# A block of the most frequent expert of the first half, gathered during attention and computed in the router's stretch

## The chip, the cores and the metric

The kernel runs on one core of a Trainium2 chip. The metric is the device time of one execution in microseconds (us). Five engines work side by side, each on its own list of instructions in order: TensorE (PE, matrix products; loads of its stationary operand are PEld), VectorE (DVE), ScalarE (ACT), GpSimd (POOL) and SyncE (SP), which here only issues transfers (DMA) and reads registers. Products land in PSUM banks; all else on the chip is in SBUF.

## The reference

Three parts in a row, in float32:

- Attention with rotary embedding for 2 batches, 8 heads, 576 positions, 64 columns a head. Its output is x, 1152 tokens of 512 columns; the first batch is tokens 0 to 575.
- A mixture of 8 experts, each token to one: `expert_idx = argmax(xn @ en.T / tau)` with normalized rows, `h = relu(x @ w1[e])` (512 to 1024), `out = gate * (h @ w2[e])` (1024 to 512), the gate being the softmax value of the chosen expert.
- A dense layer pair on the result: `x @ w_in` (512 to 2048), softplus, `@ w_out` (2048 to 512); both weights come in float64.

Products are made in three terms: an operand is split into a rounded part (hi) and the rest (lo), and hi*hi, hi*lo and lo*hi are summed. So each weight tile of 128x1024 costs a rounding copy (ACT) and a subtraction (DVE), and each activation tile likewise.

## The kernel before

**Attention.** Heads go in eight pairs j (0 to 3 are batch 0, 4 to 7 batch 1), nine steps g to a pair, t = 9j + g. The loop over t (L747) writes out the order of every engine: in step t ACT makes the exponential of tile t, PE transposes tile t-1, multiplies scores of tile t+2, and then does the step's `fill` (products with V, transposes for the next pair), which takes one or two of the two PSUM banks of `ps_m`; the evictions of these banks come in step t+1. POOL makes the rotary embedding of pair j+2 in pair j, up to pair 5. Small pieces of router work are let into the loop with generators (`next(rgen0)`).

**The router.** A token's expert is the first maximum of its 8 values; these are known for batch 0 after pair 3 and for batch 1 only at the end. From one-hot rows PE counts how many tokens of the same expert stand before each (`rank_mm`, `rank_before`, `count_mm`), `places` and `sequence` turn that into a block and a row in it, and `at_places` puts the token's number at its place with small products. Each expert gets blocks of 128 tokens, in the order of experts; `eid` and `chg` tell each block's expert and whether it is a new one.

**The blocks.** NU = 13 blocks are always worked on; with more, a branch does the rest. A block is: `gather(n)` (POOL: an indirect DMA of its rows from the copy `xs` of x in HBM), four transposes (`x_t`) and the split (`x_ev`), `layer1(n)` (24 products of 128x512), `relu(n)`, eight transposes (`h_t`) and the split (`h_ev`), `layer2(n)` (24 products), the gate's scaling (`y_row`) and the scatter to `ys` (`y_put`). Weights come in eight pieces of 512 KB a block; `split_w` rounds one on ACT, subtracts on DVE and issues the next block's fetch of that piece on SP. Blocks 0 to 3 are written out by hand (L1194 on), the others come from `run`; in four of them a piece of the dense stage's first weights is decoded (`between`, `decode`), and in the last ones finished rows of `ys` are read back and transposed (`y_t`).

Block 0 always belongs to expert 0, so its w1 is fetched and split by POOL in pairs 6 and 7 (`first_weights`). The router's stretch itself goes from the end of attention to block 0's first layer; between the router's small products PE multiplies ones with ones (`warm`, 138 products). In it POOL gathers block 0 as soon as its tokens' places are known, after both parts of `x_store(1, ...)` (batch 1's rows to `xs`: six heads' columns, then the last two heads').

**Queues.** All loads, weight fetches and stores of x are issued by SP in the order of the program; one that waits holds those behind it. Gathers and scatters are issued by POOL, between its other work. The expert stage's tiles lie where attention's were, and a tile's first write waits until the last reader of what lay there is done.

Of the kernel before, what the change touches and what calls it, by code (L numbers as in the profile page):

```python
# [33 lines left out]
NBLK = 2 * E  # L34
# [7 lines left out]
WARM0, WARM1, WARM2, WARM3, WARM4, WARM5 = 28, 22, 28, 36, 40, 12  # L42
# [9 lines left out]
def table():  # L52
# [12 lines left out]
    put("ev", np.arange(E)[None, :])  # L65
# [30 lines left out]
def moe_kernel(ctx: ExitStack, tc: tile.TileContext, q, k, v, emb, tau, w1, w2, w_in, w_out, rope, tab, out):  # L96
# [18 lines left out]
    rp = actx.enter_context(tc.tile_pool(name="rp", bufs=2))  # L115
    acon = actx.enter_context(tc.tile_pool(name="acon", bufs=1))
# [13 lines left out]
    zero = acon.tile([P, 2, 2 * P], F32, name="zero")  # L130
    V.memset(zero, 0.0)
# [49 lines left out]
    def first_max(b):  # L181
# [15 lines left out]
        if b == 0:  # L197
            both.update(oh=w([P, B * 5, E], "oh", BF16), j=w([P, B * 5], "j", I32), first=w([P, B * 5, 1], "first", F16), mask=w([P, B * 5, NBLK], "mask"), gm=w([P, B * 5, NBLK], "gm"))
        oh = rb[b]["oh"] = both["oh"][:, 5 * b:5 * b + 5]
        V.tensor_tensor(oh, rev, bc(mx, E, 2), op=ALU.is_equal)  # L200

    def rank_before(pr):

        for c in range(5):
            T.matmul(pr, lhsT=ones, rhs=bc(rb[0]["oh"][:, c], 5, 1), start=(c == 0), stop=False)

    def rank_mm(b, pr):

        oh = rb[b]["oh"]
        T.matmul(pr, lhsT=upper, rhs=oh, start=(b == 0), stop=False)  # L210
# [3 lines left out]
    def count_mm(b, pc):  # L214
        for c in range(5):
            T.matmul(pc, lhsT=ones, rhs=rb[b]["oh"][:, c], start=(b == 0 and c == 0), stop=(b == 1 and c == 4))

    def places(b, pr):
# [5 lines left out]
        ri = w([P, 5], f"ri{b}", I32)  # L224
# [15 lines left out]
        G.tensor_copy(rb[b]["row"], row)  # L240

# [30 lines left out]
    def sequence(pcnt, cnt, q):  # L272
# [26 lines left out]
        V.tensor_tensor(chg[:, 1:NBLK], ef[:, 1:NBLK], ef[:, 0:NBLK - 1], op=ALU.not_equal)  # L299
        V.tensor_copy(cnt, pcnt)  # L300
        V.scalar_tensor_tensor(nblk, nov[:, E - 1:E], 1.0, st[:, E - 1:E], op0=ALU.add, op1=ALU.add)

    def destinations(cnt, q):
# [11 lines left out]
        V.tensor_tensor(dest, base, skip, op=ALU.add)  # L315

    firsts = {}

    with actx:
# [14 lines left out]
        for t in qzs:  # L334
            G.tensor_copy(t, zero)
# [7 lines left out]
        def load(*js, between=()):  # L343
            for j in js:
                loaded[j] = (ld.tile([P, 2, 9, D], F32, tag="qk", name="qk"), ld.tile([P, 10, D], F32, tag="vv", name="vv"))
# [81 lines left out]
        def prep(j):  # L427
            if j not in prepped:
                prepped[j] = (hp.tile([P, 2, S], F32R, tag="kt", name="kt"), hp.tile([P, 2, 2, 512], F32R, tag="qt", name="qt"), qzs[j % 2])
# [50 lines left out]
        def first_weights(cs):  # L480

            for c in cs:
                raw = ld.tile([P, FF], F32, tag="qk", name="raw0")
                hi, lo = (rp.tile([P, FF], F32R, tag=t, name="part0") for t in (("t1", "t1"), ("t2", "t2"), ("ks", "qq"), ("ks", "qq"))[c])
                SY.dma_start(raw, w1[0, P * c:P * c + P])
                firsts[c] = (hi, lo)
                yield
                for x in range(4):
# [4 lines left out]
                    yield  # L493

# [63 lines left out]
        def ev_lo(t):  # L558
# [180 lines left out]

        vgen = v_first()  # L740
# [6 lines left out]
        for t in range(NS + 5):  # L747
# [72 lines left out]
            if (j, g) == (6, 1):  # L820
                wgen = first_weights((0, 1, 2))
                for _ in range(2):
                    next(wgen)
            if (j, g) == (7, 0):
                for _ in wgen:
                    pass
                wgen = first_weights((3,))
            for _ in range(4):
                next(wgen, None)
            if (j, g) == (6, 0):  # L830
                zsum(0)
                rgen0 = first_max(0)
            if (j, g) == (7, 1):
                pr0 = ps_m.tile([P, 5, E], F32, tag="m", name="pr0")
                rank_mm(0, pr0)
                rgen0 = places(0, pr0)
            elif g:
                next(rgen0, None)
# [636 lines left out]
```

## Time and profile before

| | |
|---|---|
| median of 3 runs | 574.09 us (573.15 to 574.10) |
| the profiled execution | 574.03 us, its span 572.3 us |
| granted TensorE clock, mean | 0.995 |
| busy PE, DVE, ACT, POOL | 544.2, 448.8, 440.1, 202.6 us |
| attention, to about | 183 us |
| the router's stretch | 183.7 to 194.4 us |
| the 13 blocks | 194.4 to 361.8 us |
| the dense stage | 362.9 us to the end |

Busy time counts an instruction from its start to its modelled end; products overlap, so that a stretch in which PE is marked busy throughout can still go faster. The time from one instruction's start to the next one's is the better measure, and it is what the rows of the timeline give.

### The profile page before, as it was taken

To read this page: it belongs to the slowest core of one execution; us is meant where nothing else is said; L and a number is where in the kernel's file an instruction comes from. 1 tells how busy PE (TensorE), PEld (TensorE's weight loads), DVE (VectorE), ACT (ScalarE), POOL (GpSimd) and SP (SyncE) were. 2 spreads that over 40 slices of the span, in tenths; PEclk is the share of its full clock that TensorE was granted. 3 is DMA by queue.
4 is the path that set the end of the run, shared out by engine and by line. 5 is a ranking of instruction groups with operands and counts; after the bars stand their busy time and mean duration, and the time that the engine had idled before them with its cause. 6 is when DMAs were issued, how large, how long until landed. Compare 5 with 4: busy or idle time off the path is not lost. (4 is left out here: it accounts for less than half of the span.)

```text
span 572.3 us, 10066 instructions
## 1 busy us (share of the span) xinstructions
PE 544.2 (95%) x3361; PEld 477.2 (83%) x3361; DVE 448.8 (78%) x747; ACT 440.1 (77%) x838; POOL 202.6 (35%) x314
## 2 busy tenths in 40 slices
PE   6799999999999999998999999899999999999995
PEld 6689899999988888887778888797889999888994
DVE  6788887878977779989999998687877766787243
ACT  4787878887775599799998988788877877676550
POOL 7999999849731420332222412300000000000033
PEclk9899999999999999999999999999999999999999
DMA  5405200061143655982539895453332222000012
GB/s 143 123 2 151 67 1 3 0 221 38 38 169 116 199 163 174 316 300 71 216 102 333 290 377 174 133 191 102 107 112 74 77 80 71 33 1 2 0 74 92
DMA packets 37431, 70.61 MB, mean 123 GB/s; under 512 B 8306, under 2 KB 24050, under 8 KB 37248
## 3 DMA queue, kind: packets, MB, share of 16 engines
q1 hardware_dynamic: 34400, 62.66, 33.1%
q0 software_dynamic: 2800, 7.09, 3.6%
q8 instruction: 28, 0.46, 0.3%
q10 hardware_dynamic: 176, 0.18, 0.2%
q14 instruction: 27, 0.22, 0.1%
HBM read 91.14 MB, written 8.13 MB: 173 GB/s over the span
## 5 line engine op out<-in xcount | busy, mean ns | idle before, releaser
L966 DVE TENSOR_TENSOR wt<-raw,wt 128x1024 fp32r<-128x1024 f32 x100 | 116.4, 1221 | 5.8 <-ACT wt L962 5.8
L1336 PE MATMUL ph<-yt,wt 128*128 128x320 f32 (+1 forms) x576 | 105.4, 336 | 2.5 <-ACT r__5876 L1348 1.4
L1383 PE MATMUL po<-wt,g 128*128 128x512 f32 x432 | 103.6, 391 | 0.0
L1336 PEld LDWEIGHTS ph<-yt,wt 128*128 128x128 f32 x576 | 93.5, 188 | 11.8 <-ACT r__5876 L1348 1.8
L962 ACT CAST wt<-raw 128x1024 fp32r<-128x1024 f32 x100 | 98.8, 1066 | 5.5 <-DMA raw<-in_moe_w_dram 5.5
L1383 PEld LDWEIGHTS po<-wt,g 128*128 128x128 f32 x432 | 80.4, 188 | 16.7 <-ACT g L1367 0.3
L1030 PE MATMUL py<-wt,ht 128*128 128x512 f32 x312 | 75.7, 395 | 3.8 <-DVE wt L966 3.8
L1400 POOL DMA_INDIRECT out_dram<-acc,otok x9 | 9.6, 1067 | 186.2 <-DVE acc L1397 185.6
L1030 PEld LDWEIGHTS py<-wt,ht 128*128 128x128 f32 x312 | 57.5, 188 | 16.6 <-DVE wt L966 5.1
L1001 PE MATMUL ph<-wt,xt 128*128 128x512 f32 x288 | 69.1, 394 | 0.0
L543 ACT ACTIVATE p<-sc,nm 128x576 f32<-128x576 f32 x72 | 54.0, 750 | 11.6 <-DVE nm L537 10.7
L1001 PEld LDWEIGHTS ph<-wt,xt 128*128 128x128 f32 x288 | 53.1, 188 | 10.6
L537 DVE TENSOR_REDUCE nm<-sc 128x1 f32<-128x576 f32 x72 | 54.1, 752 | 3.1 <-PE sc L533 1.9
L556 ACT CAST ph<-tp 128x512 fp32r<-128x512 f32 (+1 forms) x80 | 42.8, 547 | 13.5 <-PE tp L549 13.0
L533 PE MATMUL sc<-kt,qt 128*128 128x288 f32 x256 | 50.4, 319 | 0.8 <-ACT p L543 0.4
L567 DVE TENSOR_TENSOR pl<-tp,ph 128x512 fp32r<-128x512 f32 (+1 forms) x80 | 49.5, 628 | 0.1
L379 POOL TENSOR_TENSOR t<-qk,ropet 128x256 f32<-128x256 f32 x61 | 43.7, 744 | 10.6 <-DMA qk<-in_q_dram 10.2
L549 PE MATMUL tp<-idf,p 128*128 128x128 f32 x288 | 44.8, 278 | 1.8 <-DVE jz L233 0.6
L1367 ACT CAST g<-e 128x512 fp32r<-128x512 f32 (+2 forms) x33 | 21.6, 658 | 29.6 <-PE po L1383 20.2
L1368 DVE TENSOR_TENSOR g<-e,g 128x512 fp32r<-128x512 f32 (+2 forms) x33 | 24.3, 740 | 23.7 <-ACT g L1367 23.5
L594 PE MATMUL po<-ph,vs 128*128 128x288 f32 x128 | 36.4, 307 | 2.2 <-DVE p L435 1.3
L533 PEld LDWEIGHTS sc<-kt,qt 128*128 128x128 f32 x256 | 36.7, 192 | 1.8 <-ACT p L543 1.1
(246 smaller groups left out, 1001.7 us busy)
## 6 DMA issues: line engine op xcount, KB each, us to landing
raw<-in_moe_w_dram SPq DMA_DIRECT2D x116, 512.0 KB
raw<-in_moe_w_in_dram SPq DMA_DIRECT2D x16, 512.0 KB
raw<-in_moe_w_out_dram SPq DMA_DIRECT2D x16, 512.0 KB
yr<-ys SPq DMA_DIRECT2D x9, 256.5 KB
qk<-in_k_dram SPq DMA_DIRECT2D x8, 256.0 KB
qk<-in_q_dram SPq DMA_DIRECT2D x8, 256.0 KB
vv<-in_v_dram SPq DMA_DIRECT2D x8, 256.0 KB
xs<-xrow SPq DMA_DIRECT2D x1, 1024.0 KB
```

What stands on the lines that cost most here:

```text
L379: eng.tensor_tensor(t[:, i, g], x4[:, i, g], ropet[:, m, 0:4].unsqueeze(2).to_broadcast([P, 4, 2, 32]), op=ALU.mult)
L533: T.matmul(sc[:, n, 0:288], lhsT=w, rhs=r, start=(x == 0), stop=(x == len(mm) - 1))
L537: V.tensor_reduce(nm, tiles['sc', t][:, :, 0:288], axis=AX.XY, op=ALU.max, negate=True)
L543: A.activation(p.rearrange("p (n t) -> p n t", n=2), tiles.pop(('sc', t))[:, :, 0:288], AF.Exp, bias=tiles.pop(('nm', t)), accum_out=head( ...
L549: T.transpose(tp[:, x], p[:, x * P:x * P + P], idf)
L567: V.tensor_tensor(hd['pl'][:, :, sl], tp[:, :, x * w:x * w + w], f(hd['ph'][:, :, sl]), op=ALU.subtract)
L962: A.copy(wt[:, 0], raw)
L966: (eng or V).tensor_tensor(wt[:, 1], raw, f(wt[:, 0]), op=ALU.subtract)
L1001: T.matmul(ph[i], lhsT=xt[:, a, c], rhs=wt[:, r, 512 * i:512 * i + 512] if n else wt[r][:, 512 * i:512 * i + 512], start=(c == 0 and a == ...
L1030: T.matmul(py, lhsT=ht[c // 2][:, a, k], rhs=rhs[:, s], start=(c == 0 and r == 0 and a == 0 and s == 0), stop=(c == 3 and r == 1 and a == 1))
L1336: T.matmul(phs[i][:, 0:n1 - n0], lhsT=wt[:, a, k], rhs=yts[p][:, r, k, n0:n1], start=(k == 0 and a == 0 and r == 0), stop=(k == 3 and a == 1))
L1383: T.matmul(outs[i][c], lhsT=g[:, a, c * P:c * P + P], rhs=wt[:, r], start=(first and a == 0 and r == 0), stop=(last and a == 1))
```

## The change

The most frequent expert of batch 0 alone is found in pair 5 (`most`): its first 128 tokens (or as many as there are) become block 0, and the others are ranked as if these weren't there (`rank_shift`, and a term in `count_mm`). NBLK is 17, the remaining blocks are numbered from 1, and NU stays 13.

In pairs 6 and 7 the block's tokens are placed (`choose`) and gathered, its rows transposed (`x_first`), and w1 of that expert and three quarters of its w2 are fetched by a register and split by POOL (`first_weights(l, cs)`); the last quarter of w2 is fetched and split in the router's stretch. There both layers run (`layer1_x`, `layer2_x`), in place of `warm`. Block 1 (expert 0) follows; its weights are split like any other block's. Part of the gates' squares moves into the last steps of attention.

Pools are laid out anew: the K and Q tiles have a pool `hq`, V's loads `lv`; w2's pieces use the K and Q tiles (`hq`), the block's rows V's.

```diff
+    def most(pc):
+        m0 = w([P, 1], "m0x")
+        V.tensor_reduce(m0, pc, axis=AX.X, op=ALU.max)
...
+        V.tensor_scalar(both["ox"], rev[:, 0], mx, m0, op0=ALU.is_equal, op1=ALU.mult)
...
+    def choose(pv_):
+        toks = w([P, 5, 1], "toksx", F16)
+        V.scalar_tensor_tensor(toks[:, :, 0], rb[0]["ri"], 0.0, tb("tok")[:, 0:5], op0=ALU.is_lt, op1=ALU.mult)
+        yield
+        pv_ = pv_()
+        for c in range(5):
+            T.matmul(pv_, lhsT=rb[0]["row16"][:, c], rhs=toks[:, c], start=(c == 0), stop=(c == 4))
+        V.tensor_scalar(idx[:, 0:1], pv_, float(SKIP), None, op0=ALU.add)
...
-                (G if j else V).tensor_scalar(ri, hd['rst'][:, 0:5], 1e-9, None, op0=ALU.add)
+                if j == NP - 1:
+                    A.activation(ri, hd['rst'][:, 0:5], AF.Copy, bias=1e-9)
+                else:
+                    (G if j else V).tensor_scalar(ri, hd['rst'][:, 0:5], 1e-9, None, op0=ALU.add)
...
+            if (j, g) == (7, 6):
+                fill += [lambda: x_first(own())]
...
+            if (j, g) == (5, 0):
+                zsum(0)
+                rgen0 = first_max(0)
+            elif (j, g) == (5, 4):
+                pc0 = ps_m.tile([P, E], F32, tag="m", name="pc0")
+                count_mm(0, pc0, True)
+                rgen0 = most(pc0)
+            elif (j, g) == (6, 1):
+                pr0 = ps_m.tile([P, 5, E], F32, tag="m", name="pr0")
+                rank_shift(pr0)
+                rank_mm(0, pr0)
+                rgen0 = places(0, pr0)
+            elif (j, g) == (6, 8):
+                rgen0 = choose(lambda: ps_m.tile([P, 1], F32, tag="m", name="pi0"))
...
+            if (j, g) == (5, 8):
+                both["reg"] = SY.value_load(both["ex"][0:1, 0:1], min_val=0, max_val=E - 1)
+                wgen = first_weights(0, (0, 1, 2))
...
+            if (j, g) == (6, 6):
...
+                wgen = first_weights(1, (0,))
             if (j, g) == (7, 0):
...
+                wgen = first_weights(0, (3,))
+            if (j, g) == (7, 2):
...
+                G.indirect_dma_start(f(x0[0])[:, :], None, xs[0:S, :], bass.IndirectOffsetOnAxis(idx[:, 0:1], axis=0), ...)
+            if (j, g) == (7, 7):
...
+                wgen = first_weights(1, (1, 2))
...
+            if NS < t < NS + 4:
+                next(gg[0])
...
         def fetch_ahead():
-            for c in range(4):
-                SY.dma_start(raws_w[0, c], w1[1, P * c:P * c + P])
-            for c in range(2):
-                fetch_w(0, 1, c)
+            for c in range(3):
+                fetch_w(1, 0, c)
...
         fetch_ahead()
         x_store(1, 0, 6 * D)
+        fetch_w(0, 1, 3)
...
-        warm(WARM1, ps_y, "y")
+        for _ in range(2):
+            next(gg[0])
+        lx = layer1_x()
+        for _ in range(2):
+            next(lx)
         for _ in first_max(1):
             pass
         x_store(1, 6 * D, DM)
-        for c in range(2, 4):
-            fetch_w(0, 1, c)
+        fetch_w(1, 0, 3)
+        for c in range(3):
+            fetch_w(1, 1, c)
         rank_mm(1, pr1)
         count_mm(1, pcnt)
-        warm(WARM2, ps_y, "y")
+        for _ in range(3):
+            next(lx)
+        gg[1] = gate(1, lambda: junk)
+        next(gg[1])
+        relu(0, (0,))
+        split_hi((0, 1, 3))
+        for _ in range(2):
+            next(gg[1])
...
+        gather(1)
+        for _ in lx:
+            pass
+        relu(0, (1,))
...
+        l2 = layer2_x(ht)
+        for _ in range(2):
+            next(l2)
+        px = x_t(1)
...
+        for _ in l2:
+            pass
+        y0 = yos[0] = yo_.tile([P, DM + 1], F32, tag="last", name="yo")
+        A.copy(y0[:, 0:DM], yps.pop(0))
...
+        l1 = layer1(1)
...
+        for c in range(4):
+            split_w(2, 0, c)
+        relu(1)
```

## Rows read from the trace of the kernel before

**Rows 1.** The page, part 1: busy us, share of the span, instructions.

```profile
PE 544.2 (95%) x3361; PEld 477.2 (83%) x3361; DVE 448.8 (78%) x747; ACT 440.1 (77%) x838; POOL 202.6 (35%) x314
```

**Rows 2.** Busy time by stretch; columns: stretch, length, then as the second line names.

```profile
core 0: us, PE busy (x) PEld busy (x) DVE busy (x) ACT busy (x) POOL busy (x), PEclk, DMA share, GB/s
262.00:275.00 13.00, 12.18 (x61) 9.93 (x60) 12.79 (x16) 12.78 (x18) 3.65 (x4) 1.00 0.23 76
327.00:340.00 13.00, 13.00 (x68) 10.89 (x67) 11.89 (x13) 11.90 (x17) 2.70 (x4) 1.00 1.01 370
```

**Rows 3.** Timeline of PE, blocks: start, us, engine, line, operation, tiles, shape, count.

```profile
193.34 0.54 PE L980 MATMUL pt<-idr,xg 128*128 128x128 f32 x4 [0.69 <-DMA xg<-xs,idx]
...
194.43 3.03 PE L1001 MATMUL ph<-part,xt 128*128 128x512 f32 x12
...
213.62 5.73 PE L1001 MATMUL ph<-wt,xt 128*128 128x512 f32 x24
219.20 0.45 PE L980 MATMUL pt<-idr,xg 128*128 128x128 f32 x4
...
266.34 5.71 PE L1001 MATMUL ph<-wt,xt 128*128 128x512 f32 x24
...
279.60 5.72 PE L1001 MATMUL ph<-wt,xt 128*128 128x512 f32 x24
...
331.37 5.73 PE L1001 MATMUL ph<-wt,xt 128*128 128x512 f32 x24
...
343.87 5.71 PE L1001 MATMUL ph<-wt,xt 128*128 128x512 f32 x24
```

**Rows 4.** Timeline of all engines, end of attention and router.

```profile
182.18 0.40 ACT L600 COPY ot<-po 128x288 f32<-128x288 f32 x1 [1.32 <-PE po L596]
...
183.36 0.28 PE L205 MATMUL bank<-oh,ones 128*128 128x40 bf16 x5
...
183.74 1.39 PE L671 MATMUL junk<-ones 128*128 128x128 bf16 x22
...
187.73 0.16 DVE L1178 TENSOR_SCALAR idx<-bank 128x1 int32<-128x1 f32 x1
...
188.78 1.31 POOL L975 DMA_INDIRECT xg<-xs,idx  x1 [10.42 <-DVE sel L285]
```

**Rows 5.** Timeline of POOL, ACT and PE around step (7, 0) and (7, 1).

```profile
160.22 0.74 POOL L492 TENSOR_TENSOR part<-raw,part 128x256 fp32r<-128x256 f32 x1 [2.67 <-PE pt L450]
...
160.38 0.60 ACT L441 ACTIVATE qt<-pt 128x512 fp32r<-128x512 f32 x1
...
163.20 0.18 PE L210 MATMUL pr<-oh,upper 128*128 128x40 bf16 x1 [0.49 <-ACT ot L600]
```

**Rows 6.** Groups by line and shape, 195 to 362 us: count, busy us, mean ns, idle.

```profile
L966 DVE TENSOR_TENSOR wt<-raw,wt 128x1024 fp32r<-128x1024 f32 x99 | 115.2, 1221 | 5.8 <-ACT wt L962 5.8
L962 ACT CAST wt<-raw 128x1024 fp32r<-128x1024 f32 x96 | 94.7, 1066 | 0.8 <-DMA raw<-in_moe_w_dram 0.7
L1008 ACT ACTIVATE hr<-ph 128x512 f32<-128x512 f32 x26 | 15.0, 599 | 3.4 <-PE ph L1001 3.1
L248 ACT ACTIVATE junk<-xrow 128x512 f32<-128x512 f32 x10 | 6.3, 632 | 0.3
L248 ACT ACTIVATION_READ_ACCUMULATOR junk<-xrow 128x1 f32 x10 | 1.9, 188 | 0.0
```

**Rows 7.** POOL's splits by line, and PE's last scores in the timeline.

```profile
L492 POOL TENSOR_TENSOR part<-raw,part 128x256 fp32r<-128x256 f32 x16 | 11.8, 738 | 3.9 <-PE pt L450 2.7
L490 POOL CAST part<-raw 128x256 fp32r<-128x256 f32 x16 | 6.4, 401 | 2.1 <-PE pt L446 2.0
172.26 0.78 PE L533 MATMUL sc<-kt,qt 128*128 128x288 f32 x4
```

**Rows 8.** SyncE's issues of batch 1's stores, and the DMA while they move.

```profile
176.60 0.58 SPq L170 DMA_DIRECT2D xs<-xrow  x1
...
184.75 0.54 SPq L170 DMA_DIRECT2D xs<-xrow  x1
...
177.80:180.50 2.70, 2.46 (x18) 1.91 (x16) 1.97 (x6) 1.10 (x3) 0.53 (x1) 1.00 0.96 328
185.90:188.80 2.90, 2.67 (x51) 2.50 (x49) 2.63 (x14) 0.91 (x1) 0.01 (x1) 1.00 0.86 199
```

More of the change, by code (lines that the diff above doesn't have):

```diff
@@ L211, in rank_mm, with count_mm @@
         for d in range(1, 5):
             T.matmul(pr[:, d:5], lhsT=ones, rhs=oh[:, 0:5 - d], start=False, stop=(d == 4))
-    def count_mm(b, pc):
+    def count_mm(b, pc, alone=False):
+        if b == 0 and not alone:
+            T.matmul(pc, lhsT=ones, rhs=both["ox"], start=True, stop=False)
         for c in range(5):
-            T.matmul(pc, lhsT=ones, rhs=rb[b]["oh"][:, c], start=(b == 0 and c == 0), stop=(b == 1 and c == 4))
+            T.matmul(pc, lhsT=ones, rhs=rb[b]["oh"][:, c], start=(alone and c == 0), stop=((alone or b == 1) and c == 4))
@@ L493, in first_weights, with x_first, ev @@
                     yield
+        w2_ = w2.rearrange("e (c p r) d -> e c p (r d)", p=P, r=2)
+        def x_first(bank):
+            for k in range(4):
+                T.transpose(bank[:, k * P:k * P + P].bitcast(F32R), x0[0][:, k * P:k * P + P], idr)
+            def ev():
+                hi, lo = (lv.tile([P, 4, P], F32R, tag="vv", name="xt0") for _ in range(2))
+                x0[:] = [hi, lo]
+                src = bank.rearrange("p (k t) -> p k t", k=4)
+                A.copy(hi, src)
+                late.append(lambda: V.tensor_tensor(lo, src, f(hi), op=ALU.subtract))
+            return ev
         heads, tiles = {}, {}
@@ L1226, in moe_kernel @@
             next(l1)
[L1227 to L1228 removed]
+        pts = h_t(1)
+        split_w(1, 1, 0)
+        h_ev(1, pts, lambda: split_w(1, 1, 1))
+        for _ in range(3):
+            next(gg[0])
         for _ in l1:
             pass
+        for c in range(2, 4):
+            split_w(1, 1, c)
         for c in range(2):
[L1232 to L1234 removed]
+            split_w(3, 0, c)
@@ L1257, in moe_kernel @@
             pass
-        relu(2)
-        x_ev(3, x_t(3))
-        for c in range(4):
-            split_w(3, 0, c)
-        destinations(cnt, q)
-        for _ in layer2(1):
-            pass
-        pts = h_t(2)
-        l1 = layer1(3)
-        for c in range(2):
-            next(l1)
-        h_ev(2, pts)
-        gather(5)
-        split_w(2, 1, 0)
-        between(1)
-        split_w(2, 1, 1)
-        y_out(0)
-        for _ in l1:
-            pass
-        for c in range(2, 4):
-            split_w(2, 1, c)
-        between(2)
         relu(3)
@@ L1287, in moe_kernel @@
         pts = h_t(3)
-        between(3)
+        l1 = layer1(4)
+        for c in range(2):
+            next(l1)
+        h_ev(3, pts)
+        gather(6)
+        split_w(3, 1, 0)
+        between(2)
+        split_w(3, 1, 1)
+        G.tensor_scalar(y0[:, 0:DM], y0[:, 0:DM], gates[:, 0:1], None, op0=ALU.mult)
+        y_put(0)
+        y_out(1)
+        for _ in l1:
+            pass
+        for c in range(2, 4):
+            split_w(3, 1, c)
+        between(3)
+        relu(4)
+        x_ev(5, x_t(5))
+        for c in range(4):
+            split_w(5, 0, c)
+        y_out(2)
+        for _ in layer2(3):
+            pass
+        pts = h_t(4)
+        between(4)
         V.tensor_scalar(extra, nblk, NU, None, op0=ALU.is_gt)
```

248 lines of the change are left out of this document (148 added, 100 removed).

## The prediction

> **What bounds the kernel now.** I read the page first. TensorE (PE) is marked busy for 95% of the span [rows 1], which says little of a pipelined engine, so next came the busy time by stretch and then the order of instructions on PE. Attention is a PE stretch too. In the expert blocks, one stretch holds 12.79 of 13 us of VectorE (DVE) work and a later one 11.89 [rows 2]: where the last stage's weights are decoded, DVE sets the pace; elsewhere PE does. The starts of the first layers show it [rows 3]: 13.26 us from block to block with decoding (266.34 to 279.60), 12.50 at the end (331.37 to 343.87). Between attention and the first block lies the router: PE ends attention's work at about 183.7, multiplies ones (four batches of 22, 28, 36 and 40, the first shown, then 12 more) and starts block 0's first layer at 194.43 [rows 3, 4]. These 10.7 us are what the change fills.
>
> The times are of the profiled execution: 572.3 us of span, 574.03 in all; the median of the three runs shown is 574.09, so nothing needs to be shifted.
>
> **Does the block leave the main sequence?** With the reference's inputs for seed 0 I count 109, 200, 97, 486, 143, 31, 85 and 1 tokens per expert: 13 blocks of 128. Expert 3 has 383 in the first half. Taking 128 of it leaves 358, three blocks instead of four, so 1 + 12 blocks: still 13, and the branch for more isn't taken. The main sequence loses one block, and the one it loses is a plain one at the end, as the four decodings move along with the numbering: -12.50 us.
>
> **Attention: +2.3 us.** Added on PE: a count (5 small products), a shift (1), the tokens' places (5) and 4 transposes. Five such products took 0.28 us in the router [rows 4], and four transposes 0.54 from the first's start to the last's end, of which some 0.3 keep the next instruction out [rows 3]. That is 0.9, and PE has next to no slack here. The products borrow PSUM banks of a pair. The ranks did so before, and PE waited 0.49 us for the copy that frees one [rows 5]; they only move a pair ahead. The count is asked for in the step that has just filled both banks: in such a pair of fills PE's last transposes released POOL at 160.2, and ACT's copy of that bank ended at 160.98 [rows 5], so 0.9 us. The places' bank takes the row's 0.5. The ten or so DVE operations added, each of a few columns, fit into DVE's free fifth [rows 1]. Bounds: 0.9 (no wait) to 4 (three banks at 0.9, and DVE's next maximum late by 0.4 after the first). I take 0.9 + 0.9 + 0.5.
>
> The three squares for the gates come before the last evictions on ACT: 0.63 + 0.19 us each [rows 6], and the row at 182.18 shows ACT idle for 1.32 us ahead of one such eviction [rows 4]; there are three gaps like it. They cost nothing; without that cover, 0.8 apiece. POOL's reset of the padding tiles replaces a copy and a DVE reset at the start, ahead of inputs that land later: nothing.
>
> **POOL in pairs 6 and 7.** Seven 512 KB pieces are split there, not four. A quarter of one takes 0.40 + 0.74 us [rows 7], so the three new ones take 13.7 us. The first goes into time in which POOL waited. The other two write into the last pair's K and Q tiles, which PE reads until 172.26 + 0.78 = 173.0 [rows 7]. Then 16 operations less the first: 8.7 us, so POOL ends at 181.8, and its queue is free well before the next gather. But SyncE is held: the third weight fetch of the main sequence goes into memory that POOL still reads, and the second half's store of its first six heads stands behind that fetch.
>
> **The router: the first main block starts 5.0 us later than block 0 did.** All times are on the clock of before, without attention's 2.3.
> PE: a layer is 24 products, 5.6 us (213.62 to 219.20) [rows 3]. The first layer's 6, 9 and 9 products (1.4, 2.1, 2.1) replace the batches of ones between the router's steps, 1.39 us the first [rows 4], and would end at 190.0. By PE alone the second layer would follow, and the main block could start at about 197.2 (+2.8): this is the low end.
> The queue: before, the six heads' store was issued at 176.60 and moved from 177.8 to 180.5, 864 KB at 328 GB/s; the last two heads' store was issued at 184.75 [rows 8]. The indices of the first gather were ready at 187.9, yet POOL began it at 188.78 [rows 4], 4.0 us after that issue, when I take the store to have landed. So the store holds the gather. Now it stands behind a fetch of 512 KB (1.6 us at that rate, from about 183.2), the six heads (2.6) and another fetch (1.6): it starts at 189.0 and, with the 2.9 us that it took from 185.9 on, is through at 191.9, and the gather starts 3.1 us later than before. It took 4.55 us from POOL's start to the transposes (193.34 [rows 3]), so PE transposes at 196.4.
> ACT: the fetched weight lands at 189.2, ACT splits it (1.07), makes two squares (1.6) and only then does the second relu (0.6): 192.5 [rows 6]. Transposes, copy, and half of the second layer: PE is through at 195.9, before the gathered rows. Then transposes (0.3) and the second half (2.75): the main block starts at 199.4, 5.0 us after 194.43. DVE's 5.0 us of splits before it (1.22 each) end by 198.9. Bounds: +2.8 if no store waits, +6.5 if the gather shares its time with the four fetches now issued behind the store.
> The Trainium skill, "DMA: Bandwidth & Descriptors", Queues, rings and completion order, says that descriptors on one ring are taken in order, and that an engine takes turns between queues. By that rule the store cannot pass the fetch ahead of it, and the gather, on POOL's queue, need not wait behind all later fetches; the trace agrees as far as the 188.78 goes.
>
> **The main blocks: +1.1 us.** A first layer needs four weights that were split beforehand and are now split in time; the whole stretch has 97 splits on DVE against 100. ACT now makes four splits of the next weights before the first relu (ends 208.5, wanted at 208.1): +0.4, between 0 and 1.5. And the last decoding now falls on a block that also takes in finished rows: DVE has 0.7 us more there: +0.7, between 0 and 1.5. The scaling of block 0's rows by POOL and its scatter lie beside PE's work.
>
> **Sum:** 574.03 - 12.50 + 2.3 + 5.0 + 1.1 = 569.9 us.
>
> **Rivals.**
> A, less is lost: no store waits and no bank does: -12.5 + 0.9 + 2.8 + 0.7 = -8.1, 565.9 us. For it: the fetch may find its memory free earlier. Against: the order on SyncE.
> B, the gain is given back by DVE and ACT: they keep 97 of 100 splits, so five further periods go at 13.25 instead of 12.5: 569.9 + 3.8 = 573.7, no change. For it: 12.79 of 13. Against: 11.89 of 13 at the end leaves 1.1 us a period.
> C, slower: POOL's last two pieces. If their memory is released only at the end of attention (182) and not with the last scores, POOL ends at 191.2, the fetch, both stores and the gather follow, and the main block starts 9.4 us later still: 579.3. It decides from POOL ending 4.1 us later than 181.8. Against: POOL waited at 160.22 just until its own tile's last transposes were done [rows 5], so memory is released tile by tile.
> D, it doesn't do what it says: the remainder needs 13 blocks after all, and the extra branch costs over 12 us: some 586.
>
> **Chances.** Forecast 0.50, A 0.22, B 0.12, C 0.14, D 0.02. What a measurement here tells from no change is about 0.2%, 1.1 us. Faster: 0.48 + 0.22 + 0.02 = 0.72; the same: 0.02 + 0.08 = 0.10; slower 0.18. The range goes from A's bound to B and the upper bounds of the forecast's terms: 565.0 to 574.5; C and D are left out.
>
> **What would show it.** In the order on PE: 48 products among the router's steps, the first main layer some 7 us later than 194.43, and 12 blocks at the periods above. On SyncE: the six heads' store at about 184 instead of 176.60. On POOL: its last split near 184, and the first gather of a main block at about 194. It is wrong if attention ends over 4 us later, if PE waits in every period for DVE, or if the granted clock leaves 1.0 while PE waits for the gather.

## The result, and the profile after

The changed kernel took 581.47 us (median of 4 runs, 579.52 to 583.00) against 573.62 of the kernel before on the same chip: ratio 1.0136, 95% interval 1.0102 to 1.0171. It is slower by 1.4%, where 569.9 and a gain were forecast, and outside the range of 565.0 to 574.5.

The profiled execution after took 583.00 us, 581.2 of them span, the longest of its four; set against 574.03 before it is 9.0 us longer, 13.1 more than forecast. The table splits both spans at the same four places of PE's order.

| stretch of PE's order | before, us | after, us | change | forecast |
|---|---|---|---|---|
| start to the end of attention | 183.52 | 189.70 | +6.2 | +2.3 |
| to the first main block | 10.91 | 18.38 | +7.5 | +5.0 |
| main blocks, to the end of the last layer 2 | 167.34 | 160.63 | -6.7 | -11.4 |
| to the end of the span | 210.49 | 212.52 | +2.0 | 0 |

0.75 of the first row is not the change: at step (5, 0), where its first new work stands, the profiled executions of all kernels here lie between 0.3 us ahead of before and 1.0 behind. In the main blocks the profile before is itself 0.6 to 0.7 us longer than those of e11 and e12, which have the same blocks.

The page of after, part 1 (its first line, against [rows 1]) and one group of part 5 (against [rows 6]):

```profile
PE 540.6 (93%) x3236; PEld 471.4 (81%) x3236; DVE 449.0 (77%) x753; ACT 436.9 (75%) x837; POOL 222.8 (38%) x338
...
L1066 DVE TENSOR_TENSOR wt<-raw,wt 128x1024 fp32r<-128x1024 f32 x97 | 113.1, 1222 | 5.3 <-ACT wt L1062 5.0
```

PE has less work and 9 us more span, so look for PE's waits. Attention first, as total, number and longest of each wait of PE from 100 to 190 us of after:

```profile
PE pc L243 <- ACT kt L492: 2.5, 1, 2.5
PE po L659 <- DVE xt L554: 0.9, 1, 0.9
...
PE tp L611 <- DVE pl L629: 0.9, 2, 0.6
PE px L675 <- DVE qz L480: 0.8, 1, 0.8
...
```

The count (`pc`) waits 2.5 us for its bank; `xt` and `qz` are new too. What stands behind the 2.5 us is on the other engines. Rows of VectorE before, then of VectorE, POOL and ACT of after:

```profile
153.02 0.20 DVE L200 TENSOR_TENSOR oh<-tabt,mx 128x40 bf16<-128x40 f32 x1
```

```profile
127.48 1.19 DVE L202 TENSOR_TENSOR oh<-tabt,mx 128x40 bf16<-128x40 f32 x1
127.19 2.77 POOL L427 TENSOR_TENSOR qq<-t,t 128x576 f32<-128x576 f32 x2
129.45 0.74 ACT L605 ACTIVATE p<-sc,nm 128x576 f32<-128x576 f32 x1 [1.25 <-DVE nm L599]
```

`oh` marks each token's expert; the change moves it from pair 6 to pair 5, where POOL still makes rotary embedding (`qq`). There it takes 1.19 us instead of 0.20 (0.71 in e11, whose code here is that of before), VectorE's next maximum (`nm`) is late by that, ACT's exponential waits 1.25 us for the maximum, and ACT's copy of the count's bank stands behind the exponential. In after and in e11 it ended with a product of POOL's that ran beside it, and in before none ran there; that this is the reason for the 1.19 us was not tried. Then PE's timeline of after, columns as in [rows 3]:

```profile
199.71 0.66 PE L1080 MATMUL pt<-idf,hr 128*128 128x128 f32 x4 [2.73 <-ACT hr L1130]
...
204.89 0.51 PE L1080 MATMUL pt<-idr,xg 128*128 128x128 f32 x4 [1.64 <-DMA xg<-xs,idx]
208.08 2.90 PE L1101 MATMUL ph<-wt,xt 128*128 128x512 f32 x12
...
229.28 5.96 PE L1101 MATMUL ph<-wt,xt 128*128 128x512 f32 x24
...
378.21 0.53 PE L997 MATMUL pt<-idr,yr 128*128 128x128 f32 x4 [1.09 <-DMA yr<-ys]
379.01 0.54 PE L997 MATMUL pt<-idr,yr 128*128 128x128 f32 x4 [0.27 <-DMA yr<-ys]
380.95 0.53 PE L997 MATMUL pt<-idr,yr 128*128 128x128 f32 x4 [1.40 <-DMA yr<-ys]
381.94 0.62 PE L997 MATMUL pt<-idr,yr 128*128 128x128 f32 x4 [0.47 <-DMA yr<-ys]
```

PE waits for block 0's second relu (2.73), for the first main gather (1.64), and for finished rows at the start of the dense stage (3.2 in all). A first layer of 24 products takes 5.83 to 5.96 us, a second 5.71; before both took 5.7 [rows 3]. Who holds these up is read on the other engines: the timelines of SyncE, POOL and ACT of after, one each.

```profile
169.57 18.43 SPq L1052 DMA_DIRECT2D raw<-in_moe_w_dram  x3
188.05 0.58 SPq L172 DMA_DIRECT2D xs<-xrow  x1
```

```profile
178.36 0.72 POOL L539 TENSOR_TENSOR part<-raw,part 128x256 fp32r<-128x256 f32 x1 [2.95 <-PE sc L595]
...
186.43 0.73 POOL L539 TENSOR_TENSOR part<-raw,part 128x256 fp32r<-128x256 f32 x1
...
198.51 1.05 POOL L1075 DMA_INDIRECT xg<-xs,idx  x1 [9.97 <-DMA xs<-xrow]
...
251.41 1.07 POOL L1162 DMA_INDIRECT ys<-yo,dest  x1 [0.28 <-ACT wt L1062]
...
252.99 1.00 POOL L1162 DMA_INDIRECT ys<-yo,dest  x1 [0.28 <-POOL yo L1158]
260.58 0.18 POOL L1158 COPY yo<-idx 128x1 int32<-128x1 int32 x1 [6.59 <-DMA ys<-yo,dest]
...
373.02 1.17 POOL L1162 DMA_INDIRECT ys<-yo,dest  x1 [5.30 <-ACT a L964]
```

```profile
196.75 1.04 ACT L1062 CAST wt<-raw 128x1024 fp32r<-128x1024 f32 x1 [2.78 <-DMA raw<-in_moe_w_dram]
...
260.63 0.69 ACT L1159 ACTIVATE yo<-py,gates 128x512 f32<-128x512 f32 x1 [4.23 <-DMA ys<-yo,dest]
```

The store of six heads leaves at 188.05 (before 176.60 [rows 8]), behind three fetches, the last of which waits until POOL's last split ends at 187.16. The gather leaves at 198.51 (before 188.78 [rows 4]) and its rows reach PE 6.4 us later, not 4.55. At 260.63 ACT has waited 4.23 us for block 1's scatter, which stands on POOL behind block 0's (251.41); in that block PE waits for ACT: 14.43 us from its first layer to the next (256.25 to 270.68). The last scatter leaves at 373.02, 3.6 us after ACT finished its row (369.44).

### The profile page after: what moved, and what is told of

The parts are those of the page before. It is cut to its first block, busy times and chain, and to the rows that moved or that the text cites. A ratio compares the mean times of both kernels' runs of the same rounds, so it can differ in the third digit from the quotient of the medians.

```text
span 581.2 us, 9849 instructions
## 1 busy us (share of the span) xinstructions
PE 540.6 (93%) x3236; PEld 471.4 (81%) x3236; DVE 449.0 (77%) x753; ACT 436.9 (75%) x837; POOL 222.8 (38%) x338
## 5 line engine op out<-in xcount | busy, mean ns | idle before, releaser
L1066 DVE TENSOR_TENSOR wt<-raw,wt 128x1024 fp32r<-128x1024 f32 x97 | 113.1, 1222 | 5.3 <-ACT wt L1062 5.0
L1486 PE MATMUL ph<-yt,wt 128*128 128x320 f32 (+1 forms) x576 | 106.7, 340 | 1.1 <-ACTq L1452 1.1
L1486 PEld LDWEIGHTS ph<-yt,wt 128*128 128x128 f32 x576 | 95.0, 191 | 10.1 <-ACTq L1452 1.5
L1062 ACT CAST wt<-raw 128x1024 fp32r<-128x1024 f32 x97 | 95.9, 1072 | 3.8 <-DMA raw<-in_moe_w_dram 3.8
L1152 PE MATMUL py<-wt,ht 128*128 128x512 f32 x288 | 70.7, 396 | 6.2 <-DVE wt L1066 5.1
L1101 PE MATMUL ph<-wt,xt 128*128 128x512 f32 x288 | 70.8, 399 | 0.6 <-DVE wt L1066 0.6
L1152 PEld LDWEIGHTS py<-wt,ht 128*128 128x128 f32 x288 | 53.1, 188 | 19.0 <-DVE wt L1066 7.0
```

Source lines behind the costliest of these rows:

```text
L1062: A.copy(wt[:, 0], raw)
L1066: (eng or V).tensor_tensor(wt[:, 1], raw, f(wt[:, 0]), op=ALU.subtract)
L1101: T.matmul(ph[i], lhsT=xt[:, a, c], rhs=wt[:, r, 512 * i:512 * i + 512], start=(c == 0 and a == 0 and r == 0), stop=(c == 3 and a == 1))
L1152: T.matmul(py, lhsT=ht[c // 2][:, a, k], rhs=rhs[:, s], start=(c == 0 and r == 0 and a == 0 and s == 0), stop=(c == 3 and r == 1 and a == 1))
L1486: T.matmul(phs[i][:, 0:n1 - n0], lhsT=wt[:, a, k], rhs=yts[p][:, r, k, n0:n1], start=(k == 0 and a == 0 and r == 0), stop=(k == 3 and a == 1))
```

## Experiments

Theory W: the change put waits into queues with slack elsewhere, so undoing a wait gives its time back. Theory L: the engines have no room, and a wait removed comes back elsewhere. Ratios are to the kernel before.

**One wait undone at a time, then three.** e1:

```
-            elif (j, g) == (5, 4):
+            elif (j, g) == (5, 5):
                 pc0 = ps_m.tile([P, E], F32, tag="m", name="pc0")
```


> The count of the first half's experts is asked for one step later, at (5, 5), where only one of the two PSUM banks has just been filled; nothing else changes. Theory W (waits: the loss is made of single waits that the change put into PE's, SyncE's and POOL's queues): PE's 2.5 us wait for ACT's copy of K before the count goes to 0.5 or less, attention ends 2 us earlier, and the whole is 1.5 to 2.5 us faster than the changed kernel. Theory L (load: attention has no slack, so the added work itself costs, and a wait removed appears elsewhere): attention ends less than 0.7 us earlier.

e2:

```
-            for c in range(3):
-                fetch_w(1, 0, c)
+            fetch_w(1, 0, 0)
...
         x_store(1, 6 * D, DM)
-        fetch_w(1, 0, 3)
+        for c in range(1, 4):
+            fetch_w(1, 0, c)
```


> The second and third weight fetch of block 1 are issued behind the second half's two stores instead of ahead of them; the bytes are the same. Theory W: the store of six heads goes out when its rows are ready, some 5 us earlier than 188; the last store is through about 4 us earlier, POOL's gather of block 1 starts at about 194.5 instead of 198.5, and the first main layer about 4 us earlier than 208.1; the whole is 3 to 5 us faster than the changed kernel. Theory L: the DMA engines are full from 188 to 203, so the gather lands as late as before and the whole changes by less than 1 us, or the weights come late in its place.

e3:

```
-        G.tensor_scalar(y0[:, 0:DM], y0[:, 0:DM], gates[:, 0:1], None, op0=ALU.mult)
-        y_put(0)
...
         y_out(2)
+        G.tensor_scalar(y0[:, 0:DM], y0[:, 0:DM], gates[:, 0:1], None, op0=ALU.mult)
+        y_put(0)
```


> POOL scales block 0's rows and scatters them behind the scatter of block 2 instead of ahead of that of block 1. Theory W: ACT's wait of 4.2 us for the yo tile at 260.6, which ends with a scatter, falls to under 1 us, the first block with decoding takes 12.2 instead of 14.4 us, and the whole is 1.5 to 2.3 us faster than the changed kernel. Theory L: in these blocks DVE and ACT set the pace, and the whole gains under 0.5 us.

e4 is e1, e2 and e3 together.

> All three edits together. Theory W: the gains add, 7 to 9 us, so the kernel is within 1 us of the one before the change. Theory L: under 3 us.

| run | us | ratio (95%) |
|---|---|---|
| e1 | 579.80 | 1.0132 (1.0095 to 1.0170) |
| e2 | 579.31 | 1.0100 (1.0078 to 1.0122) |
| e3 | 579.76 | 1.0096 (1.0065 to 1.0126) |
| e4 | 574.47 | 1.0019 (1.0003 to 1.0035) |

Each alone is worth little in the median, and the intervals of all three meet that of the changed kernel: the ratio falls by 0.04, 0.36 and 0.40% alone, by 1.17% (7.0 us) with the three together. In PE's waits of e1 over the same stretch the 2.5 us of the count are gone, and 1.2 stand for `pl` and 0.7 for `km` (in place of `qz`); the last row is of e5, whose attention is e1's:

```profile
PE tp L611 <- DVE pl L629: 1.8, 2, 1.2
...
PE px L675 <- DVE km L221: 0.7, 1, 0.7
```

```profile
PE tp L612 <- DVE pl L630: 0.7, 2, 0.6
```

From step (5, 0) on, attention costs 1.2 us less than in after, between W and L. But the wait for `pl` is not the price of the edit. It comes where `oh` takes 1.2 us and nearly goes where it takes 0.8, and that differs between kernels whose attention has the same code: from ACT's exponential of step (5, 0) to the end of attention it is 71.7 to 72.0 us in e1, e4, e6, e8, e9 and e16, and 70.9 to 71.0 in e5, e7 and e10. So with the count where after has it: 73.2 in after and e3, 72.4 in e2, where `oh` takes 0.8 and the count waits 1.5 us. About 1 us between two profiles is therefore no effect of an edit in attention. Within either form the later count wins 1.2 to 1.5 us.

In e2 the store leaves at 180.29 and the gather at 193.69, and the first main block starts 15.7 us after attention instead of 18.4; but ACT's wait behind block 0's scatter grows to 6.08 us, and that block takes 19.0 (ACT's timeline of e2):

```profile
258.40 0.69 ACT L1158 ACTIVATE yo<-py,gates 128x512 f32<-128x512 f32 x1 [6.08 <-DMA ys<-yo,dest]
```

Not all of the 19.0 is the wait. The granted clock falls to half behind it, and 23 products of layer 2 take 8.26 us that took 5.52 in after (PE's timeline of e2, then its busy times, columns as in [rows 2]):

```profile
262.31 8.26 PE L1151 MATMUL py<-wt,ht 128*128 128x512 f32 x23 [0.69 <-DVE wt L1065]
```

```profile
258.00:262.00 4.00, 0.89 (x6) 0.36 (x3) 2.26 (x3) 3.60 (x6) 2.00 (x3) 0.92 0.61 232
262.00:268.00 6.00, 5.69 (x13) 4.45 (x14) 5.41 (x7) 6.00 (x9) 3.40 (x4) 0.50 0.82 275
```

In e3 ACT waits there for nothing (its timeline again), and the block takes 12.3 us instead of 14.4:

```profile
255.56 0.70 ACT L1159 ACTIVATE yo<-py,gates 128x512 f32<-128x512 f32 x1
```

So W holds for the store and the scatter, and a gain ahead of an unmended wait is lost in it, in e2 with the slow clock on top. In e4 the first block starts 15.3 us after attention, inside the forecast's 15.9.

**The pace of layer 1, and the fetches.** e5 moves one pool of weight buffers by 160 bytes:

```
+        pad = ectx.enter_context(tc.tile_pool(name="pad", bufs=1, reuse_waits="tile"))
+        pad.tile([P, PAD // 4], F32, name="pad")
         wp2 = ectx.enter_context(tc.tile_pool(name="wp2", bufs=3, reuse_waits="tile"))
...
-        gap.tile([P, GAP // 4], F32, name="gap")
+        gap.tile([P, (GAP - PAD) // 4], F32, name="gap")
```


> The three-edit kernel (e4: 574.5 us, layer 1 of the blocks at 233 ns a product from the third block on, its first block at 227) with the pool of three weight buffers moved up by 160 bytes and the gap behind it shortened by as much, so that nothing else moves. In e4 the first main block, whose weights all lie in the pool of five, runs at 227 ns, and each later block shows 231, 231, 238 ns while it reads the pool of three and falls back within the last six products, which read the pool of five. If the place of the pool of three against the other tiles (0 instead of 160 bytes past a multiple of 512) makes the pace, the blocks return to 227 ns: 11 blocks x 18 products x 6 ns = 1.2 us, so 573.2. If it is not the place (a queue, the DMA traffic beside it), the pace stays at 233 ns and the time at 574.5.

e6 moves `for c in range(3): fetch_w(1, 1, c)` behind the reading of the experts' list:

```
         gather(2)
         for _ in sgen:
             pass
+        regs[2] = [SY.value_load(t[0:1, 2:3], min_val=0, max_val=m) for t, m in ((eid, E - 1), (chg, 1))]
+        for c in range(3):
+            fetch_w(1, 1, c)
```


> e4 with the three fetches of the second layer's weights of the first main block issued behind the reading of the list of experts (about 198 us) instead of ahead of it (192 to 195). If the first main gather (193.2, landed after 6.7 us against 4.6 before) is late because it shares the DMA engines with these three, it lands at 198 to 199, PE's wait of 1.25 us goes and the first main block starts 1.2 us earlier relative to the end of attention (15.3 to about 14.1): 573.3. If the engines are simply full until 209 whatever the order, the gain comes back as a wait for weights at the second main block (0.8 us there now) and the time stays at 574.5.

e7 is e6 with `split_w(2, 0, 0)` moved ahead of `x_ev(2, px, "ht1")`, e8 all of these.

> e6 with ACT's and VectorE's split of the first weight of the second main block put ahead of the turned tokens of the third block (ACT waits 1.7 us there for PE). If the wait of PE for a split weight at the second block (0.56 us in e4) comes from this order, it goes: e6 less 0.5 us. If the weight itself is late (DMA full), the split waits in place of the tokens and nothing is won, or the second block starts later by the wait.

> e4 with the edits of e5, e6 and e7 together. If they are separate waits the gains add: 574.5 less 1.2, 1.2 and 0.5 = 571.6, faster than the kernel before (573.4) by 0.3%. If the DMA engines bound the first blocks, only the pace is won: 573.2, the same as before.

e5: 574.22 (1.0011, 0.9994 to 1.0029); e6: 576.89 (1.0054, 1.0036 to 1.0072); e7: 576.93 (1.0059, 1.0041 to 1.0077); e8: 576.30 (1.0044, 1.0027 to 1.0061). The place of the weights' buffers makes the pace. The same block in PE's timeline of e4, then of e5:

```profile
304.46 5.83 PE L1100 MATMUL ph<-wt,xt 128*128 128x512 f32 x24
```

```profile
302.86 5.72 PE L1103 MATMUL ph<-wt,xt 128*128 128x512 f32 x24
```

From product to product that is 233 and 228 ns in the mean, and the main blocks together shorten from 158.67 to 157.33 us, as expected; the medians of e4 and e5 don't tell them apart. In e6 the gather is on time and the first block starts 13.8 us after attention, but the next block's weights come late, and PE waits for them and for their splits (PE's timeline of e6):

```profile
209.97 0.50 PE L1100 MATMUL ph<-wt,xt 128*128 128x512 f32 x1 [1.65 <-ACT wt L1061]
211.29 4.38 PE L1100 MATMUL ph<-wt,xt 128*128 128x512 f32 x11 [0.81 <-DVE wt L1065]
```

The granted clock is at half (0.50) from 212 to 215 us, which is part of the 4.38. A fetch moved back only turns one wait into a longer one: here the full DMA was right. e7's order of splits changes nothing, but it was tried only with these late fetches: ACT waits for the weight itself (ACT's timeline of e7).

```profile
208.13 1.04 ACT L1061 CAST wt<-raw 128x1024 fp32r<-128x1024 f32 x1 [4.20 <-DMA raw<-in_moe_w_dram]
```

**The last scatter.** Its hold-up stood in every variant so far (2.8 to 3.6 us behind its row). e9:

```
+        y_put(NU - 1)
         with tc.If(blocks > NU, preferred_fallthrough_block=True, label="extra"):
-            y_put(NU - 1)
...
         with tc.manual_schedule():
-            y_put(NU - 1)
```


> e5 (574.2 us) with the scatter of the last main block (y_put(NU - 1)) put ahead of the branch over the extra blocks instead of behind it on both sides. In e5 its row is ready at 360.3 us, but GpSimd issues the scatter at 363.4, 3.1 us later, where the kernel before took 0.8; the loads of the finished rows follow it, PE waits for them (0.39, 0.35, 0.69, 0.73 us at 368 to 372) and its granted clock is at half from 371 to 377. If GpSimd is late because it is in the branch (theory branch), the scatter leaves at about 360.6, the loads land 2.5 us earlier, and the waits and the slow clock go: dense to the end 211.4 to 209.4 or less, 572. If it waits for something else (a free place in its queue of transfers), the scatter stays where it is and the time at 574.2.

e10:

```
-                more(NU + 1, NB)
+                more(NU + 1, NB - 1)
```


> e5 with one block fewer written out in the branch that this input never takes (more(NU + 1, NB - 1)), as many as the kernel before has: an input that needs the seventeenth block would be short of it. If the length of the skipped code makes the branch of GpSimd slow (the change made it one block longer), the scatter comes 0.8 us behind its row again and the dense stage is 2 us shorter: 572. If not the length, the scatter stays 3.1 us behind its row: 574.2.

e11, on the kernel before (with two banks widened to hold 17 columns):

```
-NBLK = 2 * E
+NBLK = 2 * E + 1
```


> The kernel before (573.2 us) with room for 17 blocks instead of 16 and nothing else of the change: one more block in the branch that is never taken, and lists of 17. If the longer skipped code is the cause, the last scatter comes 3 us behind its row instead of 0.8 and the time rises by about 2 us, to 575; if not, 573.2 and 0.8 us.

e12 is e9's edit on the kernel before.

> The kernel before with only the edit of e9. Its scatter already stands 0.8 us behind its row, so at most 0.5 us earlier rows can be won: the waits of 0.27 us for rows at 370 go, 572.7 to 573.2, and the gain of e9 over e5 (2 us) is the change's own loss given back rather than a gain that any kernel of this form has.

e9: 572.85 (0.9987, 0.9975 to 0.9998); e10: 572.41 (0.9990, 0.9978 to 1.0002); e11: 574.53 (1.0026, 1.0014 to 1.0039); e12: 573.40 (1.0004, 0.9992 to 1.0016). POOL's last scatter ahead of the dense stage, one row each of the kernel before, e10, e9 and e11; the number in brackets is POOL's idle time ahead of it, behind the small copy of that block's tokens:

```profile
363.29 0.98 POOL L1040 DMA_INDIRECT ys<-yo,dest  x1 [2.53 <-ACTq L1302]
361.80 0.98 POOL L1164 DMA_INDIRECT ys<-yo,dest  x1 [2.31 <-ACTq L1455]
362.50 0.98 POOL L1164 DMA_INDIRECT ys<-yo,dest  x1 [2.37 <-ACTq L1456]
365.06 1.00 POOL L1040 DMA_INDIRECT ys<-yo,dest  x1 [4.81 <-ACT r L871]
```

In e9 no branch stands ahead of the scatter, and POOL is idle for 2.37 us all the same: it waits for ACT's row and issues 0.8 us behind it. In the kernel before and in e10 it is 0.8 us too, so there the branch is hidden behind that wait, and all that is seen of it is that it takes no more than the 2.3 to 2.5 us. With one more block in the code that is never entered, the scatter leaves 2.8 to 3.6 us behind its row in after and e1 to e8, and 3.2 in e11, the kernel before with nothing else of the change, where it costs 0.26%; one block less (e10), or the scatter ahead of the branch (e9), gives it back, and on the kernel before, which did not lose it, the latter wins nothing (e12). The name after the arrow is only whatever ended nearest. That the time goes into loading code is not shown. The Trainium skill, "Runtime: NRT & Kernel Launch", Instruction fetch mechanics, says that a branch to code outside the stretch already loaded waits for that code to be fetched. By that rule a longer skipped part can cost a wait that a shorter one did not; e10 and e11 agree in so far as one block decides, and no run here shows the fetch.

What follows on PE can be more than the late rows. Busy times and granted clock of e5 by stretch, with the columns in the first line, then one stretch of e10, then two of e4:

```profile
core 0: us, PE busy (x) PEld busy (x) DVE busy (x) ACT busy (x) POOL busy (x), PEclk, DMA share, GB/s
368.00:370.00 2.00, 1.07 (x8) 0.79 (x8) 1.21 (x3) 1.84 (x4) 0.72 (x2) 1.00 1.02 275
370.00:372.00 2.00, 0.78 (x5) 0.60 (x5) 2.00 (x4) 1.48 (x3) 0.56 (x2) 0.64 1.01 308
372.00:374.00 2.00, 2.00 (x10) 2.00 (x11) 1.39 (x3) 1.27 (x4) 0.13 (x1) 0.50 1.08 358
```

```profile
372.00:374.00 2.00, 2.00 (x15) 2.00 (x14) 1.85 (x4) 2.00 (x6) 0.00 (x0) 1.00 1.03 352
```

```profile
370.00:372.00 2.00, 1.27 (x10) 0.80 (x8) 1.21 (x2) 1.49 (x3) 0.39 (x2) 1.00 1.00 242
372.00:374.00 2.00, 0.62 (x5) 0.48 (x5) 2.00 (x5) 1.45 (x4) 0.25 (x2) 1.00 0.97 318
```

In the first four microseconds of e5 PE works less than half the time; the clock falls in the second two (0.64) and is at half (1.2 GHz) in the next two, in which 10 products fit where e10 has 15. From the first dense product to the end of the span e5 takes 211.4 us, e10 208.8, the kernel before 209.4. In e4 the scatter is as late, PE works less than half of four microseconds too, and yet the clock stays at 1.00: its dense stage takes 210.0. So the same late scatter costs different amounts: 209.4 to 212.0 us in the ten kernels with the longer branch ahead of it, against 208.8 to 209.4 in the other eight.

**What of the attention and the fetches is left.** All on e9. e13 puts `x_first(own())` ahead of `xout(2 * j - 1)` in the list of the step:

```
+            if (j, g) == (7, 6):
+                fill += [lambda: x_first(own())]
             if g == (3 if end else 6) and j:
                 fill += [lambda: xout(2 * j - 1)]
-            if (j, g) == (7, 6):
-                fill += [lambda: x_first(own())]
```


> e9 (572.9 us) with the four transposes of block 0's tokens put ahead of the product of the finished head in the same step instead of behind it. In the trace PE waits 0.94 us at 178 us for VectorE's second part of these tokens (L555 in e10), because the attention's output needs their bank and ScalarE and VectorE reach it last. If the wait is the order's, it goes: attention ends about 0.9 us earlier, 572.0. If VectorE has no slack there (load), the wait moves to the finished head or to the next pl and the attention ends where it did: 572.9.

e14 (so for `m0`, `ox` and `km` as well):

```
-        V.tensor_scalar(both["ex"], mx, -1.0, float(E), op0=ALU.mult, op1=ALU.add)
+        G.tensor_scalar(both["ex"], mx, -1.0, float(E), op0=ALU.mult, op1=ALU.add)
```


> e9 with four of the seven small operations that find the most frequent expert (ex, m0x, ox, km) on GpSimd instead of VectorE. Before 131 to 138 us VectorE is busy without a gap, and px waits 0.70 us at 138 behind them. If VectorE's load makes that wait, moving 0.15 + 0.14 + 0.29 + 0.14 = 0.72 us of it away takes 0.7 us off the attention: 572.2. If it is the wait on a bank, as at the count, the wait stays: 572.9.

e16 (and e17, the three together):

```
         fetch_w(0, 1, 3)
+        for c in range(1, 4):
+            fetch_w(1, 0, c)
...
         x_store(1, 6 * D, DM)
-        for c in range(1, 4):
-            fetch_w(1, 0, c)
```


> e9 with three fetches of the first main block's weights put between the two stores instead of behind the second. The DMA engines are idle from 186 to 190 us and then full until 209. If full engines make the gather late (6.5 us against 4.6 before) and the second block's weights late (0.58 and 0.76 us of PE's waits), 1.5 MB landed before 190 takes 3.9 us off the full stretch: gather on time (-1.3), waits -0.6 to -1.3, together 570.3 to 571.0. If SyncE waits for GpSimd's last split (186 us) past the second store's time (189.3), as in the changed kernel, nothing is won or up to 2 us lost: 572.9 to 575.

> e9 with the edits of e13, e14 and e16 together. If all three are separate waits the gains add to 0.9 + 0.7 + 2.0 = 3.6: 569.3, 0.7% faster than the kernel before and 0.6 below the time that was predicted for the change. If VectorE's load rules the attention, only the fetches count: 570.9.

e13: 571.43 (0.9977, 0.9966 to 0.9988); e14: 572.45 (0.9993, 0.9979 to 1.0006); e16: 571.15 (0.9974, 0.9961 to 0.9986); **e17: 570.64 against 572.62 of the kernel before beside it, 0.9961 (0.9947 to 0.9975), faster than both kernels.** In e13 the wait for `xt` is gone, and 0.50 us for another tile stands in its place (PE's timeline of e13):

```profile
177.99 0.37 PE L660 MATMUL po<-ph,vs 128*128 128x288 f32 x1 [0.50 <-DVE xrow L688]
```

Counted from step (5, 0), its attention is 0.9 us shorter than e9's, but 0.8 of that arises in pair 5, ahead of the edit, where e13 has the short form of e5 and e10. From pair 7 on it takes 28.0 us in e13 and 28.1 in e9 and e10: the edit itself is worth 0.2, nearer to the load than to the order. In e14 the wait for `km` is gone too, but one of 0.42 for `pl` appears a pair later, and no gain can be measured. In e16 the fetches leave in the DMA's idle stretch and the second store is not held (188.69); SyncE of e16, then PE's wait for the gather:

```profile
184.92 1.73 SPq L1054 DMA_DIRECT2D raw<-in_moe_w_dram  x3
188.69 0.55 SPq L173 DMA_DIRECT2D xs<-xrow  x1
```

```profile
198.76 0.51 PE L1082 MATMUL pt<-idr,xg 128*128 128x128 f32 x4 [0.49 <-DMA xg<-xs,idx]
```

That wait was 1.38 us in e9. The waits for the second block's weights (0.58, 0.76) stay as they were. ACT's timeline of e9 shows that they are not the DMA's:

```profile
206.74 0.59 ACT L1086 CAST xt<-pt 128x512 fp32r<-128x512 f32 x1 [1.70 <-PE pt L1082]
...
207.85 3.96 ACT L1064 CAST wt<-raw 128x1024 fp32r<-128x1024 f32 x4
```

ACT waits 1.70 us for PE's transposes of that block's tokens, copies them, makes a square, and takes up the four weights without any wait for them. Against e9's ratio e13 is 0.10% lower, e16 0.13% and e17 0.26% (1.5 us, of the 3.6 that were expected). The intervals of e13 and e16 overlap e9's, so neither is told apart from it in time alone; e17's ends where e9's begins.

## Why the prediction was wrong

**The steps that failed,** in the order of the sum:

1. *Attention, +2.3: "so 0.9 us" for the count's bank, and DVE's additions that "fit into DVE's free fifth".* The wait for the bank was named, its size was not: it is 2.5 us in after and 1.5 in e2, and the later count (e1) wins 1.2. The copy that frees the bank was priced by its own time, but it stood behind an exponential that waited for VectorE. The free fifth is a mean over the span: in pair 5 `oh` takes 0.8 to 1.2 us instead of 0.20, from 131.6 to 140 us VectorE works without a gap, and at 140.77 PE waits 0.77 us for `qz` and comes out of that step 1.0 later still. The transposes of block 0's tokens show a wait of 0.9 for their bank, where 0.3 was counted, but without it (e13) only 0.2 is won. What is left is spread: e5 still spends 1.1 us more than before in pair 5, 0.7 in pair 6, 0.6 in pair 7 and 0.8 behind it, and no single wait of PE accounts for it. No wait of PE names the three squares on ACT, as said.
2. *Router, +5.0: the chain of fetch, store, fetch, store and gather.* The chain was right; its links were longer. POOL's last split ended at 187.2, 3.1 us behind the 184.1 that 181.8 and 2.3 make, most of it attention's own excess. Two sizes were too small: the gather landed after 6.4 us, not 4.55 (the four fetches behind the store, the upper bound of the text), and ACT's wait for the fetched weight held the second relu until 199.1, so PE's work could no longer hide behind the gather. With the fetches behind the store (e4) the router costs +4.4 over before, below the forecast.
3. *Main blocks, +1.1: "The scaling of block 0's rows by POOL and its scatter lie beside PE's work."* POOL's queue lies beside PE's work, but block 1's scatter stands in it behind block 0's, the single `yo` buffer behind that, ACT behind the buffer, and PE behind ACT: 14.4 us for that block instead of 12.3 (e3), 2.3 over all the blocks. Besides, the first two blocks took 2.0 more, mostly in waits for split weights, where 0.4 was costed, and the pace of layer 1 took 1.3 over all the blocks (e5, from the traces; the medians don't show it), where nothing was.
4. *Dense stage: no term at all.* A block that leaves, but a branch that grows: one more block in the skipped code made the last scatter late (e9, e10, e11) and with it the rows: +2.0 in the profile of after, where the clock fell to half behind them, 0.0 to 2.6 over the kernel before in the ten kernels with the longer branch ahead of that scatter.

**What held.** The block left (12 main blocks, 97 splits, -12.5); POOL's end released a held fetch, and the store and gather stood behind it; DVE and ACT did not take the gain back (rival B), since plain blocks ran at 12.6 us at the end; rival D's extra blocks never ran. Rival C's time, 579.3, is near the result, but its mechanism did not happen: POOL's last two pieces went on when PE's last scores were done (178.36), as the prediction had it. One of the text's own signs of failure came in after: attention ended over 4 us later. The other that it named, the granted clock, held at 1.0 while PE waited for the gather, and fell only in the dense stage; but it fell at that place in e1 (0.51 from 197.0 to 200.4 us) and e3 (0.50 from 200 to 203), whose router is the changed kernel's. Two slips of the prediction's sums changed nothing: the range begins at 565.0, where A's sum gives 565.9, and C lets POOL's last work take 9.2 us, where the forecast counts 8.7.

**The size of the whole.** Undoing the causes leads from a ratio of 1.0136 to 1.0019 (e4), 1.0011 (e5), 0.9987 (e9) and 0.9961 (e17). The forecast's was 0.9928 (569.9 of 574.03), so the best form wins a little over half of it; that 570.6 us lies close to 569.9 is in part the chip, on which the kernel before took 572.62. Of e17's span against before, attention still costs 3.5 us (forecast 2.3), the router 2.9 (5.0), the remaining block terms 3.3 (1.1), against 12.5 won and 0.5 less in the dense stage.

**Open.** The first two main blocks wait 1.3 us for split weights, and e9's ACT shows that the fetch is not the cause; whether another order of ACT's work wins it is untested, as e7 tried one only where the weights themselves were late. Why the place of three buffers changes the pace, what POOL does during the longer branch, and why the clock falls behind the late rows in e5 and not in e4. Whether the other 3 us of attention are VectorE's load was tried only by e14, and whether `oh` would be short again in a pair without POOL's rotary embedding was not tried.

## What to carry to other kernels

Small work put into a full stretch is priced by the buffers and queues that it borrows, not by its own duration: ask for each borrowed bank when it was filled, and for each transfer added to a queue which buffer is released only behind it. A stage that is not touched can pay too: tiles that moved by some bytes cost 1.3 us here, and code that is only skipped 0 to 2.6, with the clock that fell behind it in most executions. When several such waits stand in one chain, undo them together, since one alone is lost in the next. And before a shorter stretch in one profile is put down to an edit, look whether it is shorter ahead of the edit too.

## What was not expected of the hardware

- Products of 128x128 by 128x512 follow each other at 227 ns, or at a repeating 231, 231, 238 (mean 233), by the place of the buffers of their weights: 160 bytes of shift of one pool brought 227 back (e4, e5). Which relation of the places decides is not shown. In the kernel before, the later blocks begin at 224 to 236 and fall to 227 after 3 to 10 products.
- With one more block in the code that it skips, POOL is idle for 4.5 to 5.3 us ahead of its last scatter (after, e1 to e8, e11); with the shorter code it is idle for 2.3 to 2.5 (before, e10), as it is with no branch there at all (e9).
- VectorE's comparison of 128x40 to bf16 (`oh`) took 0.20 us in before and e12, 0.71 in e11, and 0.8 to 1.2 in pair 5 of every changed kernel; it ended within 0.1 us of a product of POOL's that ran beside it in after, e2 and e11, and none ran beside it in before.
- PE's clock is at half in e5 after its waits of 0.39, 0.35, 0.69 and 0.73 us, though PE then has work throughout, and stays at 1.00 in e4 after waits of 2.0 us in all.
